# The loop of a gated attention-and-expert kernel, turned: the next tile's scores first, then q, u and the output

## The chip, the cores and the metric

The kernel runs on one core of one Trainium2 chip. The metric is the device time of one execution in microseconds (us). A core has five engines that each work through their own instructions in order: TensorE (PE in the profile; its weight loads are PEld), VectorE (DVE), ScalarE (ACT), GpSimd (POOL) and SyncE (SP, which here only issues DMAs). They wait for one another through semaphores. The tile library inserts those waits from the data that instructions share, and from the reuse of buffers; in this kernel each engine's order is the order in which the program writes its instructions.

## The reference

Two branches over the same input x (2048 rows of 512) are mixed by a gate per row.

```
g = sigmoid((x * gate_w).sum(-1))
# A: linear attention, 32 heads of 16
q, k, v = heads(x @ wqkv)
phi(y)  = concat(softmax(y @ w_phi), softmax(-(y @ w_phi)))      # 32 features per head
kv, z   = phi(k)^T v, sum over rows of phi(k)
a       = (phi(q) kv / (phi(q) z + 1e-6)) @ wo
# B: 32 heads, each picks one of 256 experts
s1, s2  = scores of x with 2 x 16 keys per head
e       = argmax(s1) * 16 + argmax(s2)
b       = sum over heads of gelu(x . u[e]) * v[e]                # softmax over one candidate is 1
out     = g * a + (1 - g) * b
```

## The kernel before, in words

Rows are handled in 16 tiles of 128. Matrix products are made of three products of a high and a low part each (`mm3`, L51 to L56), so a 128x512 output with 512 inputs takes 12 matmuls.

The first part of the program (to L336) projects k and v for every tile, takes the softmax features of k and sums up kv and z. It also folds the expert keys into the score weights (`sh`, `sl`) and `w_phi` into the q weights. The last lines of it already compute the scores of tile 0. kv and z of the last two tiles are finished after it, v of the last two tiles only in the second iteration of the loop.

The second part is the loop over tiles. One tile t goes through these steps, spread over three iterations:

- `front_s` (L225): the scores, two halves of 12 matmuls (tiles `s`).
- `best` (L441): VectorE finds the maximum of each head's 16 scores and marks where it is (`mx`, `eq`, L447 and L448). `turn_eq` (L451) has SP issue a DMA that transposes the marks (`et`).
- `mid_mask` (L505): 8 small matmuls turn the marks into bit masks. `count` (L515) is a chain of 17 steps on VectorE that counts, for each of the 256 experts, how many heads picked it (L519 to L553). It is a generator: `step(t, n)` issues its next n steps, `drain(t)` the rest, so that the chain can be laid between other instructions.
- `front_q` (L386): q with `w_phi` in it, 12 matmuls (`pq`). `soft_in` (L391) makes the four VectorE operations of `softmax_diffs` (L90 to L96), `soft_exp` (L400) the exp in two halves on ScalarE (L403), `soft_w` (L405) the products with z on GpSimd (`w`, L409), `soft_sum` and `soft_y` the sums over each head's features on VectorE (L413 and L417), and `soft_b` (L419) the small operations that end in one factor per feature group (L423 to L433), with a `step` of the count behind each of them, and the scaling of the features by it on GpSimd (`d`, L439).
- `planes` (L467) and `join` (L477): the scaled features are transposed by two DMAs per tile, on 16-bit halves: ScalarE splits (`pl`, L472), SP issues the transposes (`tp`), ScalarE joins (`pt`, L482).
- `front_p` (L350): x with all 256 expert vectors u and with the gate vector, 12 matmuls of 258 columns (`pp`). `gelu_pre` (L356), `gate`, `gelu_in`, `gelu_act`, `gelu_out`: gelu and gate on ScalarE, VectorE and GpSimd. `coef` (L555) multiplies the count with it (`cf`).
- `mid_num` (L485) and `num_lo`: the numerator from `pt` and kv, with its high and low part (`oh`, `ol`). `back_c` (L559) and `back_cl`: transposes of the coefficients (`CT`, `ch`, `cl`).
- `back_o`, `back_ol`, `back_out` (L573 to L595): the output product of 18 matmuls over `wo` and the expert vectors v (`po`). `store` copies it and issues its DMA.

PSUM gives the products two rotating sets: four buffers `mm` (scores, q, u, coefficient transposes, output) and three `tr` (numerator, masks). A product has to wait until the one four places earlier in its set has been read.

In the order before, iteration a of the loop (L642) handles tile z = a-2 in its numerator and output, b = a-1 in its transposes and the rest of its count, a in its q and softmax, and n = a+1 in its scores and u. TensorE's order in it is: numerator of z, coefficient transposes of z, q of a, output of z, masks of a, scores of n, u of n. The last tile's q and the last outputs are written out behind the loop (L710 to L758).

The weights `wo` are loaded and split into `wbh` and `wbl` in the second iteration, because these two buffers hold the weights of v until then (L669, L690, L701 and L706).

Of the kernel before, what the change touches and what calls it, by code (L numbers as in the profile page):

```python
# [33 lines left out]
def mix_kernel(ctx, tc, xT, wqT, wkT, wv, wphi, wo, wq, kk, ug, ev, cst, out):  # L34
# [306 lines left out]
    def step(t, n=1):  # L341
        for _ in range(n):
            if t in chains and next(chains[t], None) is None:
                del chains[t]

    def drain(t):
        while t in chains:
            step(t)

    def front_p(t, evict=True):  # L350
        pp = st8[t]["pp"] = mm_bank(f"pp{t}")
        proj(pp[:, :NU], t, uh, ul, 0, NU)
        if evict:
            gelu_pre(t)

    def gelu_pre(t):  # L356
        pp = st8[t]["pp"]
        gs = w2.tile([P, 4], F32, name=f"gs{t}", tag="gs")
        act.activation(gs[:, 0:1], pp[:, NX:NX + 1], AF.Exp, scale=-1.0)
        act.activation(gs[:, 1:2], gs[:, 0:1], AF.Copy, bias=1.0)  # L360
        px = w2.tile([P, NX], F32, name=f"px{t}", tag="px")
        x2 = w2.tile([P, NX], F32, name=f"x2{t}", tag="x2")
        act.copy(px, pp[:, :NX])
        act.activation(x2, pp[:, :NX], AF.Square)
        act.activation(x2, x2, AF.Copy, bias=GELU_C, scale=0.044715 * GELU_C)
        st8[t].update(g=gs, G=px, x2=x2)

    def gate(t):
        gs = st8[t]["g"]
        yield dve.reciprocal(gs[:, 2:3], gs[:, 1:2])  # L370

    def gelu_in(t):
        px, x2 = st8[t]["G"], st8[t]["x2"]
        pool.tensor_tensor(x2, x2, px, op=ALU.mult)

    def gelu_act(t):
# [3 lines left out]
        act.activation(x2, x2, AF.Identity, bias=gs[:, 3:4], scale=gs[:, 3:4])  # L380
# [19 lines left out]
    def soft_exp(t):  # L400
        d = st8[t]["ph"]
        for s_ in halves:
            act.activation(d[:, s_], d[:, s_], AF.Exp)  # L403
# [63 lines left out]
    def planes(t):  # L467
        e = st8[t]
        e["tp"] = []
        for i, s_ in enumerate(halves):  # L470
            pl = w3.tile([P, 2, 512], U16, tag="pl", name=f"pl{i}_{t}")
            act.copy(pl, e["ph"][:, s_].bitcast(U16).rearrange("p (c j) -> p j c", j=2))  # L472
# [32 lines left out]
    def mid_mask(t):  # L505
        e = st8[t]
        o = tr_bank(f"mk{t}")[:, :64]
        for half in range(2):
            for w in range(2):
                for q in range(2):  # L510
                    pe.matmul(o[:, half * 32 + w * F:half * 32 + w * F + F], e["et"][:, half * 4 + w * 2 + q, :],
                              wm[:, q, :], start=(q == 0), stop=(q == 1))
        chains[t] = count(t, o)
# [100 lines left out]
    def z_final():  # L614
        for j in range(2):
            o = mm_bank(f"z{j}")
            for g in range(4):
                pe.matmul(o[:, g * P:(g + 1) * P], zc[:, 4 * j + g:4 * j + g + 1].to_broadcast([P, P]), ident,
                          start=True, stop=True)
            act.copy(zb[:, 512 * j:512 * j + 512], o)  # L620

    def wo_load(ks):
        for k in ks:
            rawo[k] = w3.tile([P, D], F32, tag="ot", name=f"rawo{k}")
            sp.dma_start(rawo[k], wo[:, k, :])

    rawo = {}
    kvz(NT - 2)
    best(0, 0)
    best(0, 1)  # L630
    cb.close()
    w3 = ctx.enter_context(tc_pool("w3", "left"))
    turn_eq(0)
    front_q(0)
    soft_in(0)
    front_p(0, False)
    kvz(NT - 1)
    act.copy(zc, acc[:, :, F])
    gelu_pre(0)
    z_final()  # L640
    wo_load((0, 1))
    for a in range(NT - 1):  # L642
        n, b, z = a + 1, a - 1, a - 2
        B, Z = b >= 0, z >= 0
        if Z:
            mid_num(z)
            back_c(z)
        if B:
            planes(b)
            front_q(a)  # L650
        if a == 1:
            v14, v15 = vproj(NT - 2), vproj(NT - 1)
        gelu_in(a)
        if Z:
            num_lo(z)
            back_cl(z)
        for _ in gate(a):
            step(b)
        gelu_act(a)
        if B:  # L660
            step(b, 4)
            soft_in(a, lambda: step(b, 2))
            drain(b)
        if a == 1:
            v14()
        soft_exp(a)
        if a == 1:
            v15()
            for k in range(2):  # L669
                act.copy(wbh[:, k, :], rawo[k])  # L670
        if Z:
            back_o(z)
            back_ol(z)
            back_out(z)
            store(z)
        mid_mask(a)
        front_s(n, 0)
        if a == 1:
# [4 lines left out]
        front_s(n, 1)  # L683
        front_p(n, False)
        soft_w(a)
        soft_sum(a, 0)
        soft_sum(a, 1)
        if a == 1:
            for k in range(2):
                pool.tensor_tensor(wbl[:, k, :], rawo[k], wbh[:, k, :], op=ALU.subtract)  # L690
            wo_load((2, 3))
        best(n, 0)
        soft_y(a, 0)
        soft_y(a, 1)
        if B:
            join(b)
            gelu_out(b)
            coef(b)
        if a == 1:
            kv_final()  # L700
            for k in range(2, NK):  # L701
                act.copy(wbh[:, k, :], rawo[k])
        soft_b(a)
        if a == 1:
            for k in range(2, NK):
                pool.tensor_tensor(wbl[:, k, :], rawo[k], wbh[:, k, :], op=ALU.subtract)  # L706
        best(n, 1)
        turn_eq(n)
        gelu_pre(n)
    a, b, z = NT - 1, NT - 2, NT - 3  # L710
    mid_num(z)
    back_c(z)
    planes(b)
    front_q(a)
    gelu_in(a)
    gelu_out(b)
    num_lo(z)
    back_cl(z)
    for _ in gate(a):
        step(b)  # L720
    gelu_act(a)
    step(b, 4)
    soft_in(a, lambda: step(b, 2))
    drain(b)
    coef(b)
    back_o(z)
    back_ol(z)
    join(b)
    soft_exp(a)
    back_out(z)  # L730
    store(z)
    mid_mask(a)
    soft_w(a)
    soft_sum(a, 0)
    soft_sum(a, 1)
    mid_num(b)
    back_c(b)
    num_lo(b)
    back_cl(b)
    soft_y(a, 0)  # L740
    soft_y(a, 1)
    gelu_out(a)
    soft_b(a)
    back_o(b)
    back_ol(b)
    back_out(b)
    mid_phi(a)
    store(b)
    drain(a)
    coef(a)  # L750
    mid_num(a)
    num_lo(a)
    back_o(a)
    back_c(a)
    back_cl(a)
    back_ol(a)
    back_out(a)
    store(a)  # L758


def _consts():
# [49 lines left out]
```

## Time and profile before

| | us |
|---|---|
| median of three executions (389.7 to 391.84) | 389.85 |
| profiled execution | 389.51 |
| its span, first to last instruction | 387.7 |
| PE busy | 379.2 (98%) |
| DVE busy | 324.3 (84%) |
| ACT busy | 214.2 (55%) |
| POOL busy | 155.9 (40%) |
| DMA | 45.38 MB, mean 117 GB/s |

The profile is one execution of the program, recorded by the hardware. A row of a timeline gives the start in us from the span's beginning, the duration, the engine, the program's line, the operation, the tile that it writes and those that it reads, and how many instructions were merged; in brackets stands how long the engine sat idle before it and what released it. Rows of windows give the length of a stretch, then each engine's busy time with the number of instructions, the granted TensorE clock as a share of the full one, and the DMA's share and rate. Matmuls are pipelined, so a row's duration is longer than the distance to the next.

### The profile page before, as it was taken

How to read it: one execution, taken by the hardware profiler on the slowest of the kernel's cores; microseconds unless marked ns; L12 is line 12 of the kernel's file. 1: busy time of each engine (PE TensorE's matmuls, PEld its weight loads, DVE VectorE, ACT ScalarE, POOL GpSimd, SP SyncE). 2: the span in 40 equal slices, each digit the busy share in tenths (PEclk: the TensorE clock that was granted, in tenths of full speed). 3: DMA queues.
4: the chain of work that ended last, by engine and by line, in shares of the span. 5: the costliest groups of instructions: out<-in, count | busy, mean ns of one | idle time of the engine just before them, and what ended most of it. 6: DMA issues, size and time to landing. Idle time of an engine off the chain costs nothing.

```text
span 387.7 us, 9193 instructions
## 1 busy us (share of the span) xinstructions
PE 379.2 (98%) x3688; PEld 296.4 (76%) x3688; DVE 324.3 (84%) x798; ACT 214.2 (55%) x390; POOL 155.9 (40%) x165
## 2 busy tenths in 40 slices
PE   8999999999999999999999999999999999999975
PEld 4866787777768888877878878888888788888753
DVE  4358866866868969889999999999999999999994
ACT  4335555644646345758548458557656664674732
POOL 1005435325326233936426426336335344364350
PEclk9999999999999999999999999999999999999989
DMA  7489787487692033143252231331440431322301
GB/s 272 157 257 313 210 254 231 142 227 238 199 300 57 16 71 81 61 78 81 57 83 60 77 81 50 88 83 34 104 83 28 90 84 48 81 69 69 83 28 56
DMA packets 66715, 45.38 MB, mean 117 GB/s; under 512 B 58096, under 2 KB 58992, under 8 KB 64368
## 3 DMA queue, kind: packets, MB, share of 16 engines
q1 hardware_dynamic: 65808, 43.92, 41.5%
q10 hardware_dynamic: 864, 0.87, 0.8%
q8 instruction: 29, 0.48, 0.5%
q14 instruction: 14, 0.11, 0.1%
HBM read 26.43 MB, written 4.19 MB: 79 GB/s over the span
## 4 chain that ended last, share of the span: by engine, by line
PE 83%; DVE 8%; ACT 3%; DMA 2%; POOL 2%; issue 1%; ACTq 0%; POOLq 0%
PE s L54 7%; PE s L56 6%; PE s L55 6%; PE pk L54 4%; PE ws L204 4%; PE pk L55 4%; PE pk L56 4%; PE pv L54 4%; PE po L578 4%; PE po L579 4%; PE po L584 3%; PE pv L55 3%; PE pv L56 3%; PE pq L54 3%; PE pq L56 3%; PE pq L55 3%
## 5 line engine op out<-in xcount | busy, mean ns | idle before, releaser
L409 POOL TENSOR_TENSOR w<-d,zb 128x512 f32<-128x512 f32 x32 | 40.8, 1299 | 94.6 <-ACT d L403 94.6
L181 POOL TENSOR_TENSOR d<-d,st 128x1024 f32<-128x1024 f32 x16 | 31.0, 1939 | 74.5 <-DVE st L180 38.4
L54 PE MATMUL s<-sh,xh 128*128 128x512 f32 x128 | 51.8, 405 | 0.0
L56 PE MATMUL s<-sh,xl 128*128 128x512 f32 x128 | 50.0, 391 | 0.0
L55 PE MATMUL s<-sl,xh 128*128 128x512 f32 x128 | 49.9, 390 | 0.0
L403 ACT ACTIVATE d<-d 128x512 f32<-128x512 f32 x32 | 18.4, 624 | 56.9 <-DVE d L96 56.9
L439 POOL TENSOR_TENSOR d<-d,st 128x512 f32<-128x512 f32 x31 | 32.7, 1077 | 25.6 <-DVE st L433 20.8
L482 ACT COPY pt<-tp 128x1024 uint16<-128x1024 uint16 x30 | 39.0, 1368 | 1.5 <-DMA tp<-pl 0.9
L326 ACT ACTIVATE d<-d 128x1024 f32<-128x1024 f32 x16 | 17.0, 1063 | 27.9 <-DVE d L96 27.9
L472 ACT COPY pl<-d 128x1024 uint16<-128x1024 uint16 x30 | 30.5, 1061 | 1.6 <-POOL d L439 1.4
L56 PEld LDWEIGHTS s<-sh,xl 128*128 128x128 f32 x128 | 24.0, 188 | 5.4
L413 DVE TENSOR_REDUCE st<-d 128x32 f32<-128x512 f32 x32 | 20.5, 681 | 8.9 <-ACT d L403 8.9
L54 PEld LDWEIGHTS s<-sh,xh 128*128 128x128 f32 x128 | 24.0, 188 | 4.6
L55 PEld LDWEIGHTS s<-sl,xh 128*128 128x128 f32 x128 | 24.1, 188 | 4.5
L578 PE MATMUL po<-wbh,oh 128*128 128x512 f32 x64 | 26.4, 412 | 0.8 <-ACT oh L496 0.8
L54 PE MATMUL pv<-wbh,xh 128*128 128x512 f32 x64 | 26.3, 411 | 0.2 <-ACT wbh L48 0.2
L54 PE MATMUL pq<-wah,xh 128*128 128x512 f32 x64 | 26.5, 415 | 0.0
L579 PE MATMUL po<-wbl,oh 128*128 128x512 f32 x64 | 26.2, 409 | 0.0
L55 PE MATMUL pv<-wbl,xh 128*128 128x512 f32 x64 | 25.4, 396 | 0.2 <-DVE wbl L49 0.2
L179 DVE TENSOR_REDUCE st<-d 128x64 f32<-128x1024 f32 x16 | 19.5, 1218 | 7.0 <-ACT d L326 7.0
L54 PE MATMUL pk<-wah,xh 128*128 128x512 f32 x64 | 25.3, 395 | 0.0
L56 PE MATMUL pv<-wbh,xl 128*128 128x512 f32 x64 | 25.2, 394 | 0.0
(147 smaller groups left out, 1019.9 us busy)
## 6 DMA issues: line engine op xcount, KB each, us to landing
wq<-wq SPq DMA_DIRECT2D x16, 1024.0 KB, 5.9
xr<-xT SPq DMA_DIRECT2D x15, 256.0 KB, 6.1
y<-ot SPq DMA_DIRECT2D x15, 256.0 KB, 2.0
rawk<-wkT SPq DMA_DIRECT2D x1, 1024.0 KB, 6.5
rawq<-wqT SPq DMA_DIRECT2D x1, 1024.0 KB, 4.8
rawo<-wo SPq DMA_DIRECT2D x4, 256.0 KB, 3.7
rawu<-ug SPq DMA_DIRECT2D x2, 258.0 KB, 6.0
rawv<-wv ACTq DMA_DIRECT2D x2, 256.0 KB, 4.6
```

The costliest lines, as they stand in the source:

```text
L54: pe.matmul(o, ah, bh, start=(first and i == 0), stop=False)
L55: pe.matmul(o, ah, bl, start=False, stop=False)
L56: pe.matmul(o, al, bh, start=False, stop=(last and i == n - 1))
L179: dve.tensor_reduce(st[:, 64:128], g64(d), axis=AX.X, op=ALU.add)
L181: pool.tensor_tensor(g64(d), g64(d), b64(st[:, 128:192]), op=ALU.mult)
L409: pool.tensor_tensor(e["w"][:, s_], e["ph"][:, s_], zb[:, s_], op=ALU.mult)
L413: dve.tensor_reduce(e["st"][:, 64 + 32 * i:96 + 32 * i], g64(e["ph"])[:, 32 * i:32 * i + 32], axis=AX.X, op=ALU.add)
L439: eng.tensor_tensor(g64(d)[:, gs_], g64(d)[:, gs_], r[:, gs_].unsqueeze(2).to_broadcast([P, 32, F]), op=ALU.mult)
L472: act.copy(pl, e["ph"][:, s_].bitcast(U16).rearrange("p (c j) -> p j c", j=2))
L482: act.copy(p16[:, :, 4 * i:4 * i + 4, :], e["tp"][i].rearrange("p (j g) n -> p j g n", j=2))
L578: pe.matmul(po, oh[:, k, :], wbh[:, k, :], start=(k == 0), stop=False)
L579: pe.matmul(po, oh[:, k, :], wbl[:, k, :], start=False, stop=False)
```

## The change

The order of the calls in the loop is rewritten; no operation on the tiles is added or left out. There is one loop over all 16 tiles, k, with z = k-2, b = k-1 and n = k+1. TensorE's order in an iteration becomes: numerator of z, coefficient transposes of z, masks of k, scores of n, q of k, u of k, output of z. Thus u is computed in the iteration of q, one later than before, and the output is last.

On VectorE, the iteration begins with `soft_b` of b, which had ended the iteration before it, and with the last steps of b's count. The count of k is placed behind the two calls of `best`: 7 steps after the first, 5 after the second, and the last 5 between the operations of `soft_b` in the next iteration. q's differences have no steps between them any more, and nothing stands between the sums of the exp and those over w but the gate's reciprocal before the last one. On GpSimd, `gelu_in`, `gelu_out` and `coef` of b follow the scaling of b's features, and `w` of k comes last. On ScalarE, `join` of b comes before the exp of k, and `gelu_pre` of k after it.

In the first iteration the sums for z (`kvz`, `z_final`) come after scores, q and u. The first half of `wo` is split in iteration 1 behind `join`, the second half in iteration 2 behind `join`. The last iteration has no scores; it takes `join` behind the exp, with four count steps ahead of it.

```diff
+    def back(t):
+        back_o(t)
+        back_ol(t)
+        back_out(t)
+        store(t)
+
+    def wo_split(ks):
+        for k in ks:
+            act.copy(wbh[:, k, :], rawo[k])
+            pool.tensor_tensor(wbl[:, k, :], rawo[k], wbh[:, k, :], op=ALU.subtract)
+
     rawo = {}
-    kvz(NT - 2)
     best(0, 0)
     best(0, 1)
...
-    for a in range(NT - 1):
-        n, b, z = a + 1, a - 1, a - 2
-        B, Z = b >= 0, z >= 0
+    for k in range(NT):
+        n, b, z = k + 1, k - 1, k - 2
+        B, Z, N, last = b >= 0, z >= 0, n < NT, k == NT - 1
         if Z:
             mid_num(z)
             back_c(z)
         if B:
+            mid_mask(k)
+        if N:
+            front_s(n, 0)
+            front_s(n, 1)
+        if B:
+            soft_b(b)
+            drain(b)
             planes(b)
-            front_q(a)
...
+            gelu_in(b)
+            gelu_act(b)
         if Z:
             num_lo(z)
             back_cl(z)
-        for _ in gate(a):
-            step(b)
-        gelu_act(a)
         if B:
-            step(b, 4)
-            soft_in(a, lambda: step(b, 2))
-            drain(b)
-        if a == 1:
+            gelu_out(b)
+            coef(b)
+        if k == 1:
+            v14, v15 = vproj(NT - 2), vproj(NT - 1)
             v14()
...
+            kv_final()
+        front_q(k)
+        if N:
+            best(n, 0)
+            step(k, 7)
+            best(n, 1)
+            turn_eq(n)
+            step(k, 5)
+        else:
+            step(k, 2)
+        front_p(k, False)
+        if k == 0:
+            kvz(NT - 2)
+            kvz(NT - 1)
+            mid_mask(0)
+        if B and not last:
+            join(b)
+        if k == 1:
+            wo_split((0, 1))
             wo_load((2, 3))
...
+        if k == 2:
+            wo_split((2, 3))
+        soft_in(k)
+        soft_exp(k)
+        if k == 0:
+            step(0, 12)
+            act.copy(zc, acc[:, :, F])
+            z_final()
+        if last:
+            step(k, 4)
             join(b)
...
+        gelu_pre(k)
+        soft_w(k)
+        soft_sum(k, 0)
+        soft_sum(k, 1)
+        soft_y(k, 0)
+        for _ in gate(k):
+            pass
+        soft_y(k, 1)
+        if Z:
+            back(z)
+    a, b = NT - 1, NT - 2
     mid_num(b)
     back_c(b)
+    gelu_in(a)
+    gelu_act(a)
     gelu_out(a)
     soft_b(a)
     back_o(b)
+    num_lo(b)
+    back_cl(b)
     mid_phi(a)
     drain(a)
     coef(a)
+    back_ol(b)
     mid_num(a)
+    back_c(a)
+    back_out(b)
+    store(b)
     num_lo(a)
     back_cl(a)
+    back(a)
```

More of the change, by code (lines that the diff above doesn't have):

```diff
@@ L633, in mix_kernel @@
     turn_eq(0)
[L634 to L640, printed above, removed]
     wo_load((0, 1))
-    for a in range(NT - 1):
-        n, b, z = a + 1, a - 1, a - 2
-        B, Z = b >= 0, z >= 0
+    for k in range(NT):
+        n, b, z = k + 1, k - 1, k - 2
+        B, Z, N, last = b >= 0, z >= 0, n < NT, k == NT - 1
         if Z:
@@ L648, in mix_kernel @@
         if B:
+            mid_mask(k)
[5 more added lines that the diff above has]
+            drain(b)
             planes(b)
-            front_q(a)
-        if a == 1:
-            v14, v15 = vproj(NT - 2), vproj(NT - 1)
-        gelu_in(a)
+            gelu_in(b)
+            gelu_act(b)
         if Z:
@@ L656, in mix_kernel @@
             back_cl(z)
-        for _ in gate(a):
-            step(b)
-        gelu_act(a)
         if B:
-            step(b, 4)
-            soft_in(a, lambda: step(b, 2))
-            drain(b)
-        if a == 1:
+            gelu_out(b)
+            coef(b)
+        if k == 1:
+            v14, v15 = vproj(NT - 2), vproj(NT - 1)
             v14()
-        soft_exp(a)
-        if a == 1:
             v15()
[L669 to L678, printed above, removed]
             kvacc(NT - 2)
@@ L682, in mix_kernel @@
             w4 = ctx.enter_context(tc_pool("w4", "right"))
[L683 to L690, printed above, removed]
-            wo_load((2, 3))
[L692 to L695, printed above, removed]
-            join(b)
[L697 to L735, printed above, removed]
+            kv_final()
[13 more added lines that the diff above has]
+            mid_mask(0)
@@ L736, in mix_kernel @@
+        for _ in gate(k):
[4 more added lines that the diff above has]
+    a, b = NT - 1, NT - 2
     mid_num(b)
     back_c(b)
[L738 to L741, printed above, removed]
+    gelu_in(a)
+    gelu_act(a)
     gelu_out(a)
@@ L744, in mix_kernel @@
     back_o(b)
-    back_ol(b)
-    back_out(b)
+    num_lo(b)
+    back_cl(b)
     mid_phi(a)
-    store(b)
     drain(a)
     coef(a)
+    back_ol(b)
     mid_num(a)
+    back_c(a)
+    back_out(b)
+    store(b)
     num_lo(a)
-    back_o(a)
-    back_c(a)
     back_cl(a)
-    back_ol(a)
-    back_out(a)
-    store(a)
+    back(a)
 def _consts():
```

## The prediction, made before the changed kernel ran

> **What bounds the kernel now.** I read the page's engine totals, then a window of one iteration, then the chain of work that ended last.
>
> ```profile
> span 387.7 us, 9193 instructions
> PE 379.2 (98%) x3688; PEld 296.4 (76%) x3688; DVE 324.3 (84%) x798; ACT 214.2 (55%) x390; POOL 155.9 (40%) x165
> ...
> 337.02:352.16 15.14, 15.14 (x109) 12.31 (x110) 14.13 (x42) 9.18 (x18) 6.77 (x7) 1.00 0.30 70
> ...
> PE 83%; DVE 8%; ACT 3%; DMA 2%; POOL 2%; issue 1%; ACTq 0%; POOLq 0%
> ```
>
> The third row is one iteration, from the first score product of one to that of the next: length, then busy time of PE, PEld, DVE, ACT, POOL, and behind them the granted clock. TensorE has no gap in it, and the last row, the chain's shares, puts 83% of the span on TensorE. The second number to see is VectorE's 14.13 of 15.14: the next engine has about 1 us to spare. The change adds and removes no arithmetic, so TensorE's work of 15.14 per iteration stays. A new order can only change how long TensorE idles at the start and in the tail, or push a round of another in-order engine above 15.14. So I worked out VectorE's round. Its timeline in one iteration before, with the two rows of ScalarE and GpSimd that it waits for:
>
> ```profile
> 321.94 0.68 DVE L96 TENSOR_TENSOR d<-st,pq 128x512 f32<-128x512 f32 x1
> ...
> 323.32 1.28 DVE L413 TENSOR_REDUCE st<-d 128x32 f32<-128x512 f32 x2 [0.36 <-ACT d L403]
> 324.79 0.69 DVE L447 TENSOR_REDUCE mx<-s 128x32 f32<-128x512 f32 x1 [0.19 <-PE s L56]
> ...
> 326.12 1.27 DVE L417 TENSOR_REDUCE st<-w 128x32 f32<-128x512 f32 x2
> 327.31 0.54 DVE L423 RECIPROCAL st<-st 128x64 f32<-128x64 f32 x1
> ...
> 328.96 0.19 DVE L523 TENSOR_TENSOR sa<-sb 128x64 uint16<-128x64 uint16 x1
> 329.06 0.69 DVE L447 TENSOR_REDUCE mx<-s 128x32 f32<-128x512 f32 x1
> ...
> 330.62 0.76 DVE L503 TENSOR_TENSOR ol<-oT,oh 128x256 fp32r<-128x256 f32 x2
> ...
> 331.69 0.37 DVE L527 TENSOR_TENSOR m<-sa 128x32 uint16<-128x32 uint16 x2
> ...
> 332.71 0.29 DVE L542 TENSOR_SCALAR T<-X 128x256 uint32<-128x256 uint32 x1
> ...
> 333.71 0.68 DVE L90 TENSOR_REDUCE st<-pq 128x32 f32<-128x512 f32 x1
> 334.31 0.28 DVE L545 TENSOR_SCALAR X<-X 128x256 uint32<-128x256 uint32 x1
> ...
> 322.65 1.16 ACT L403 ACTIVATE d<-d 128x512 f32<-128x512 f32 x2 [3.73 <-DVE d L96]
> ...
> 323.36 2.56 POOL L409 TENSOR_TENSOR w<-d,zb 128x512 f32<-128x512 f32 x2 [6.60 <-ACT d L403]
> ```
>
> The reader is to see a latency that is partly covered. The last difference of q ends at 322.62; the exp starts 0.03 later, the first sum of its result 0.70 later (323.32), and GpSimd's products w end at 325.92, which is 3.30 after 322.62. Before, the last count step and best(n,0) (L447 and L448, 324.79 to 326.12) fill that time, so the sums over w (326.12) wait for nothing.
>
> **The change, part by part.** *TensorE's order* becomes num, coefficient transposes, masks, scores of the next tile, q, u, output. Same matmuls, so 0 by itself.
>
> *VectorE's round* (from one L423 to the next) is where I see the cost. The count no longer runs between q's differences, and best(n,0) no longer stands between the sums and the w sums. By start-to-start distances:
> (a) soft_b with count steps 13 to 17 in it. Soft_b with steps 1 to 5 takes 1.75 (327.31 to 329.06). The later steps are longer; alone they take 1.70 in the tail:
>
> ```profile
> 377.20 0.29 DVE L542 TENSOR_SCALAR T<-X 128x256 uint32<-128x256 uint32 x1
> ...
> 379.11 0.29 DVE L547 TENSOR_TENSOR T<-X 128x256 uint16<-128x256 uint16 x1
> ...
> 380.81 0.42 DVE L557 TENSOR_TENSOR cf<-cf,px 128x256 f32<-128x256 f32 x1
> ```
>
> Bounds 1.75 and 1.75+1.70-0.5 = 2.95 (0.5 being five of the 0.10 from 328.96 to 329.06). I take 2.25: two chains that fill each other's latencies, as in the row they replace.
> (b) num_lo and back_cl, 1.00 of the 1.07 from 330.62 to 331.69.
> (c) best twice, 2 x 1.33 = 2.66.
> (d) count steps 1 to 7 with nothing between: the five small ones cost 0.5 (pipelined at 0.10) to 1.3 (1.75 less 0.46 for L423, as if they were all of it). I take 1.0, dependent operations of under 0.2 each; steps 6 and 7 are 331.69 to 332.71, 1.02. Together 2.0.
> (e) steps 8 to 12 alone, 377.20 to 379.11, less 0.1 where best's end overlaps: 1.8.
> (f) q's four differences without steps between, 4 x 0.60 (333.71 to 334.31), to the end of the last: 2.48.
> (g) from there 3.30 to the end of w, 0.05 to react and 0.60 for the last w sum: 3.95. Only 2.5 of it is work (two sums 1.2, two w sums 1.2, the gate's reciprocal); about 1.45 is idle, where 0.36 was before.
> Sum: 2.25+1.00+2.66+2.0+1.8+2.48+3.95 = **16.14**, already 1.0 above TensorE's 15.14.
>
> *What GpSimd adds to that.* In the second iteration before, GpSimd runs beside count steps:
>
> ```profile
> 159.15 0.69 DVE L425 TENSOR_TENSOR st<-st 128x64 f32<-128x64 f32 x1
> 159.77 0.74 DVE L520 TENSOR_TENSOR sb<-sa 128x64 uint16<-128x64 uint16 x1
> ...
> 193.05 0.19 DVE L520 TENSOR_TENSOR sb<-sa 128x64 uint16<-128x64 uint16 x1
> ...
> 159.71 0.75 POOL L384 TENSOR_TENSOR px<-x,px 128x256 f32<-128x256 f32 x1
> ...
> 329.12 2.08 POOL L439 TENSOR_TENSOR d<-d,st 128x512 f32<-128x512 f32 x2 [1.68 <-DVE st L433]
> ```
>
> L520 takes 0.74 until just after GpSimd's product ends (160.46), against 0.19 when GpSimd is idle. In the new round soft_b comes first, so GpSimd's two halves of d (2.08) and gelu_in (of L384's size, 0.75) run from 2.0 (or 2.3, if the last count step holds them) to 5.2 after its start, and steps 2 to 7 begin at about 4.9 (a+b+one best+one step): about 0.3 more. Bounds 0 and 1.0, two whole products. **Round 16.4**; bounds 15.6 (a at 2.0, d at 1.55, no blocking) and 17.2.
>
> The Trainium skill ("SBUF — State Buffer", SBUF: two separate sides) says that VectorE and GpSimd share one port pair as an exclusive lock, held for a whole instruction, by a VectorE operation with two SBUF inputs or in a two-port mode. The rows above agree for two inputs. By that rule the one-input step 8 would also wait for GpSimd's coefficient product, some 0.25 more per round by the 0.74 rows, which no row here shows; the sum would be 414 with it.
>
> *What stands behind.* If VectorE is late by 1.2 each iteration, TensorE waits: the next scores take the PSUM buffer of q, free only when q's differences are done. ScalarE and SP hold no longer loop:
>
> ```profile
> 331.01 2.02 ACT L472 COPY pl<-d 128x1024 uint16<-128x1024 uint16 x2
> ...
> 333.47 0.60 ACT L380 ACTIVATE x<-x,gs 128x256 f32<-128x256 f32 x1
> ...
> 324.18 2.60 ACT L482 COPY pt<-tp 128x1024 uint16<-128x1024 uint16 x2
> ...
> tp<-pl SPq DMA_TRANSPOSE x4, 2.8
> ```
>
> Planes start 3.4 after soft_b's start, the transpose of the first half lands 1.0+2.8 later, join takes 2.6: done at about 10, while the exp queued behind it is due at 12.2 (a to f). It is hidden; with that cover of 2 gone it would add what it exceeds.
>
> *The start.*
>
> ```profile
> 137.57 0.47 PE L54 MATMUL s<-sh,xh 128*128 128x512 f32 x1
> ...
> 143.09 0.28 PE L54 MATMUL pp<-uh,xh 128*128 128x258 f32 x1
> ...
> 144.51 0.40 PE L54 MATMUL pq<-wah,xh 128*128 128x512 f32 x1
> ...
> 152.77 0.36 PE L511 MATMUL mk<-wm,et 128*128 128x16 bf16 x8
> ...
> 155.95 1.27 PE L188 MATMUL kvacc<-v,d 128*32 128x16 f32 x128
> ...
> 164.02 2.57 POOL L706 TENSOR_TENSOR wbl<-rawo,wbh 128x512 fp32r<-128x512 f32 x2
> ...
> 192.33 0.55 DVE L423 RECIPROCAL st<-st 128x64 f32<-128x64 f32 x1
> ```
>
> Before, TensorE has done q(1), v14 and v15 at 152.77. In the new order q(1) comes after scores(2) (5.52, from 137.57 to 143.09), a mask and both kv sums too, less u(1) (1.42): 152.77+5.52+0.2+1.3-1.42, and 0.9 waiting for the z copy, now queued behind an exp: 159.3. VectorE idles for it some 4 us. q's differences end at 161.8. GpSimd's two wo remainders (2.57) now stand before w in both k=1 and k=2 and hold it up by about 0.9 and 0.65; so the L423 of tile 1 is at 166.65, of tile 2 at 183.7. The first output product waits for wo's second half, split only behind join(1), until about 180, TensorE idling some 8 us; that delays scores(4) by 0 to 2 beyond VectorE's need, I take 0.9. The L423 of tile 3 falls at 201.0, against 192.33.
>
> *The tail.*
>
> ```profile
> 357.60 0.55 DVE L423 RECIPROCAL st<-st 128x64 f32<-128x64 f32 x1
> ...
> 373.02 0.54 DVE L423 RECIPROCAL st<-st 128x64 f32<-128x64 f32 x1
> ```
>
> Before, from the L423 of tile 14 to that of 15 takes 15.4, and 14.7 more to the end, 30.1 together. New: no scores, so q's differences end 6.1 after the first; but w waits behind gelu_out and coef on GpSimd. These follow the planes and gelu on ScalarE (3.06 from 331.01 to 334.07, so until 6.6) and take two 0.75, to 8.2; w ends at 10.8, and the last sum at 11.4; 11.9 with steps blocked beside it. From the last L423 the old 14.7, and 1.2 because the last coefficient transposes and tile 14's six closing matmuls now precede the whole last output product: 15.9. Together 27.8, a gain of 2.3.
>
> *Sum.* 201.0 + 11 x 16.4 + 27.8 = 409.2 of span. The profiled execution took 389.51 for 387.7, so 1.8 outside: **411**. It lies 0.34 under the median of the runs shown, which changes nothing here.
>
> **Rivals.** (1) *Count steps hide better*: round 15.6, the low bound. For it: soft_b's 0.10 steps. Against: the steps are a chain with nothing between them now. 411 - 11 x 0.8 = 402.
> (2) *GpSimd blocks more*: one more whole product of 0.74 per round, since gelu_out and coef fall beside steps 7 and 8. 411 + 11 x 0.75 = 419.
> (3) *TensorE's clock drops in the new gaps.*
>
> ```profile
> 370.65:374.00 3.35, 3.35 (x9) 2.62 (x10) 3.24 (x11) 0.50 (x2) 2.42 (x3) 0.55 0.21 81
> ```
>
> The granted clock there is 0.55, after TensorE's sparse stretch before. 3.35 x 0.45 = 1.5 lost per drop makes TensorE's round 16.65 plus reaction, say 16.8: 415. Against: the gaps are 1.2 long and the granted clock of the iteration row is 1.00. The Trainium skill ("TensorE: Matmul & The Clock Gate", Part 1) has the clock halve after an idle window of about 3.4 us; by it neither gap of 1.2 would trip it, and the tail's row agrees with a drop after a longer quiet stretch.
> (4) *TensorE stays the bound* (the other side): VectorE's round comes to 15.14 or less. Place: (d) and (g); price: 1.26 a round; point: round 15.14. Then TensorE's own work sets the end: tile 13's output product, before one iteration behind 352.16 at about 367.1, comes later only by what TensorE idles at the start, 1.1 (z) to 9.5 (with the wait for wo). From there it is 17.3 by the tail's terms (q(15) is done 5.8 earlier, then 2.5+4.3+15.9, rounded up by 0.4 for the reaction), and 1.8 outside: 387 to 396, middle 391.5, no longer slower by more than 0.5% below 5.6 of idling. For it: VectorE's 14.13. Against: (g)'s idle 1.45 comes on top.
>
> **How the numbers follow.** Forecast 53%, rival 1 20%, rival 2 12%, rival 3 5%, rival 4 10%. The range 397 to 420 leaves out most of rival 4 and a little above rival 2. A measurement of this kernel tells 0.5% (2 us) from no change. Faster and same come from rival 4 alone, its 387 to 391.8, half of its chance, and as much again for errors of the start in rivals 1 and 4: 0.05 and 0.06; slower 0.89.
>
> **What would show it.** In the profile after: TensorE's first score product waiting about 1 us per iteration for L96; L417 waiting for w, L413 for the exp with 0.7; iterations 16 to 17 long; DVE near 14.5 busy in them; L520 long where L374 runs; an 8 us gap before the first L578. Wrong if iterations are 15.1 with TensorE gapless, or if the waits before L417 are missing.

## The result, and the profile after

The changed kernel takes **412.65 us** (median of four executions, 411.29 to 413.34); the kernel before, run beside it, takes 389.77. The ratio is 1.057 with a 95% interval of 1.0525 to 1.0616. The profiled execution took 412.62 for a span of 410.8, which is 23.1 longer than before.

The page of the changed kernel: span and instructions, busy time of each engine, the TensorE clock in 40 slices of the span, and the shares of the chain that ended last.

```profile
span 410.8 us, 9252 instructions
PE 385.3 (94%) x3688; PEld 299.3 (73%) x3688; DVE 329.9 (80%) x798; ACT 216.4 (53%) x390; POOL 156.5 (38%) x165
...
PEclk9999999999999989969999999999999999999969
...
DVE 42%; PE 37%; POOL 10%; issue 3%; DMA 3%; ACT 3%; ACTq 0%; POOLq 0%; DVEq 0%
```

The instructions of the engines are the same in number, but TensorE has fallen from 83% of the chain to 37%, and VectorE leads it with 42%. The clock row is full in the loop and drops only near the middle (the start of the loop) and in the last slices.

To see where the 23.1 us went, I cut both spans at the same two events: the reciprocal L423 of tile 3 and that of tile 14. Windows of the kernel before between these two (busy time of PE, PEld, DVE, ACT and POOL, then the granted clock):

```profile
192.33:357.60 165.27, 165.27 (x1178) 134.08 (x1177) 155.88 (x452) 101.34 (x198) 74.78 (x78) 1.00 0.31 71
```

The same stretch after, and one typical round of it:

```profile
204.57:380.38 175.81, 170.30 (x1203) 137.98 (x1201) 157.10 (x453) 103.16 (x198) 75.41 (x77) 1.00 0.35 67
284.34:300.29 15.95, 15.28 (x110) 12.41 (x109) 14.25 (x42) 9.49 (x18) 6.85 (x7) 1.00 0.32 67
```

Up to tile 3 the changed kernel loses 12.24 (204.57 against 192.33), in the eleven rounds 10.54 (175.81 against 165.27), and behind them 0.32 (410.8 - 380.38 = 30.42 against 30.1). A round takes 15.98 on average, in which TensorE idles 0.50 and VectorE 1.70 (175.81 - 157.10 over 11). VectorE was idle 0.85 per round before (165.27 - 155.88 over 11), so 0.85 of the 0.96 by which a round is longer is new idle time of VectorE.

VectorE's timeline in the typical round, from one L423 to the next:

```profile
284.34 0.54 DVE L423 RECIPROCAL st<-st 128x64 f32<-128x64 f32 x1
...
286.41 0.75 DVE L503 TENSOR_TENSOR ol<-oT,oh 128x256 fp32r<-128x256 f32 x2
...
287.40 0.68 DVE L447 TENSOR_REDUCE mx<-s 128x32 f32<-128x512 f32 x1
...
288.72 0.21 DVE L519 CAST sa<-mk 128x64 uint16<-128x64 f32 x1
...
290.73 0.69 DVE L447 TENSOR_REDUCE mx<-s 128x32 f32<-128x512 f32 x1
...
292.06 0.34 DVE L542 TENSOR_SCALAR T<-X 128x256 uint32<-128x256 uint32 x1
...
293.89 0.68 DVE L90 TENSOR_REDUCE st<-pq 128x32 f32<-128x512 f32 x1
...
295.69 0.67 DVE L96 TENSOR_TENSOR d<-st,pq 128x512 f32<-128x512 f32 x1
297.06 1.28 DVE L413 TENSOR_REDUCE st<-d 128x32 f32<-128x512 f32 x2 [0.70 <-ACT d L403]
298.44 0.69 DVE L417 TENSOR_REDUCE st<-w 128x32 f32<-128x512 f32 x1
...
299.69 0.69 DVE L417 TENSOR_REDUCE st<-w 128x32 f32<-128x512 f32 x1 [0.49 <-POOL w L409]
300.29 0.55 DVE L423 RECIPROCAL st<-st 128x64 f32<-128x64 f32 x1
```

The reader is to see two idle stretches, 0.70 ahead of L413 and 0.49 ahead of the second L417. Both stand in the latency from q's last difference over the exp and GpSimd's products back to VectorE, which nothing on VectorE fills any more. The sums of all such waits between 200 and 370 us (in total, times, longest):

```profile
DVE st L413 <- ACT d L403: 7.7, 11, 0.7
DVE st L417 <- POOL w L409: 5.4, 11, 0.5
PE s L54 <- DVE d L96: 3.1, 5, 0.7
```

The first two come in every round; the third is TensorE's first score product, which waits for the buffer that q's differences free. It comes in only 5 of the 11: TensorE enters these rounds ahead of VectorE, and its first score products follow one another by 15.10 up to 233.08, then by about 16. VectorE is late, and TensorE waits for it once its lead is used up.

### The profile page after: what moved, and what is told of

Same layout as the page of the kernel before. It is cut to its first block, busy times and chain, and to the rows that moved or that the text cites. A ratio compares the mean times of both kernels' runs of the same rounds, so it can differ in the third digit from the quotient of the medians.

```text
span 410.8 us, 9252 instructions
## 1 busy us (share of the span) xinstructions
PE 385.3 (94%) x3688; PEld 299.3 (73%) x3688; DVE 329.9 (80%) x798; ACT 216.4 (53%) x390; POOL 156.5 (38%) x165
## 4 chain that ended last, share of the span: by engine, by line
DVE 42%; PE 37%; POOL 10%; issue 3%; DMA 3%; ACT 3%; ACTq 0%; POOLq 0%; DVEq 0%
POOL w L409 8%; DVE eq L448 4%; PE pv L54 4%; DVE mx L447 4%; PE ws L204 3%; PE pk L54 3%; PE pv L55 3%; PE pk L55 3%; PE pk L56 3%; PE pv L56 3%; DVE st L417 2%; ACT d L403 2%; DVE ol L503 2%; DVE st L90 2%; DVE d L96 2%
## 5 line engine op out<-in xcount | busy, mean ns | idle before, releaser
L578 PE MATMUL po<-wbh,oh 128*128 128x512 f32 x64 | 27.1, 423 | 4.9 <-ACT wbh L635 4.2
L417 DVE TENSOR_REDUCE st<-w 128x32 f32<-128x512 f32 x32 | 21.9, 684 | 9.1 <-POOL w L409 7.9
L413 DVE TENSOR_REDUCE st<-d 128x32 f32<-128x512 f32 x32 | 20.4, 680 | 9.8 <-ACT d L403 9.8
L579 PE MATMUL po<-wbl,oh 128*128 128x512 f32 x64 | 27.1, 423 | 0.6 <-POOL wbl L636 0.6
L54 PE MATMUL pq<-wah,xh 128*128 128x512 f32 x64 | 25.4, 398 | 0.4 <-DVE d L96 0.4
```

The lines of the kernel that those rows point to most:

```text
L54: pe.matmul(o, ah, bh, start=(first and i == 0), stop=False)
L417: dve.tensor_reduce(e["st"][:, 192 + 32 * i:224 + 32 * i], g64(e["w"])[:, 32 * i:32 * i + 32], axis=AX.X, op=ALU.add)
```

## The experiments

**Fill the exp's latency.** Two of the five count steps behind `best(n, 1)` are put between q's differences and the sums of the exp.

```diff
-            step(k, 5)
+            step(k, 3)
...
         soft_in(k)
         soft_exp(k)
+        if N:
+            step(k, 2)
```

> Two of the five count steps that stand ahead of q's differences (L545 and L546, 0.67 us together in the profile after) move behind them, into the 0.70 us in which VectorE waits for the exp. Theory, VectorE's own round sets the pace and its idle time counts in full: the round falls from 15.96 by 0.67 to 15.3 us, over some 12 rounds 8 us, about 404.6 in all. Rival, the pace is set elsewhere (TensorE with a lowered clock, GpSimd, a transfer): no change, 412.6.

Measured: 404.46 (403.27 to 405.41), ratio to before 1.0363 (1.0337 to 1.0389), span 401.5. Its window between the same two events, and its VectorE timeline at the place of the edit:

```profile
203.50:371.11 167.61, 167.61 (x1197) 137.09 (x1196) 156.09 (x452) 103.19 (x199) 75.21 (x77) 1.00 0.34 70
```

```profile
290.60 0.29 DVE L545 TENSOR_SCALAR X<-X 128x256 uint32<-128x256 uint32 x1
290.93 0.43 DVE L546 TENSOR_TENSOR X<-X,T 128x512 uint16<-128x512 uint16 x1
291.39 1.28 DVE L413 TENSOR_REDUCE st<-d 128x32 f32<-128x512 f32 x2
```

L413 waits for nothing here, and eleven rounds take 167.61 instead of 175.81, so 15.24 each, with TensorE busy throughout (its own iterations take 15.10). Putting 0.79 us of existing work (290.60 to 291.39) back into the gap gave 8.2 us between the two events. Most of the 13.8 us of span that stay against the kernel before lie ahead of tile 3 (203.50 against 192.33); 2.34 lie in the eleven rounds.

**Fill the latency of the products w instead.** The same two steps stand between `soft_sum` and `soft_y`.

```diff
-            step(k, 5)
+            step(k, 3)
...
         soft_sum(k, 1)
+        if N:
+            step(k, 2)
         soft_y(k, 0)
```

> The same two count steps move to the place between the sums of the exp and the first sum over w, where VectorE waits 0.1 and 0.5 us for GpSimd's products. If only idle time counts, about 0.5 us of a round is saved, 6 us in all, 406 to 407. If VectorE's step and GpSimd's product exclude each other (the products run there back to back, 1.28 us each), the second step ends only with the second product, the sums over w follow late by 0.65, and nothing is gained: 412 to 413.

Measured: 415.2 (414.81 to 416.03), ratio 1.0643 (1.0621 to 1.0664): no gain, and the eleven rounds are 1.28 longer (177.09). VectorE at that place:

```profile
299.60 1.40 DVE L546 TENSOR_TENSOR X<-X,T 128x512 uint16<-128x512 uint16 x1
300.92 0.67 DVE L417 TENSOR_REDUCE st<-w 128x32 f32<-128x512 f32 x1
```

L546 takes 1.40 against 0.43 elsewhere, because it runs beside a product of GpSimd (w, 298.12 to 300.72), and the sums over w stand behind it. The gap is there, but only work that can run beside GpSimd fits into it.

**An operation that does fit.** The reciprocal of the sums, first of `soft_b`, is moved ahead of the first sum over w.

```diff
+    def soft_r(t):
+        st = st8[t]["st"]
+        dve.reciprocal(st[:, 128:192], st[:, 64:128])
...
-        dve.reciprocal(r, sm)
         step(t)
...
         soft_sum(k, 1)
+        soft_r(k)
         soft_y(k, 0)
```

> The reciprocal of the sums (L423, 0.46 us of the round) moves from behind the sums over w to the place ahead of them. It reads one small tile. Theory: it fills the 0.6 us of waiting for w, the round falls by 0.46 to 15.5 us, 5.5 us in all, about 407. If a reciprocal too has to wait for GpSimd's products, it ends up to 1.2 later and nothing is gained: 412 or more.

Measured: 406.38 (405.9 to 406.94), ratio 1.0413 (1.0389 to 1.0436), span 404.8. The reciprocal (L421 here) beside GpSimd's w:

```profile
294.03 0.56 DVE L421 RECIPROCAL st<-st 128x64 f32<-128x64 f32 x1
...
295.34 0.69 DVE L417 TENSOR_REDUCE st<-w 128x32 f32<-128x512 f32 x1
```

Its duration is about that of L423 (0.54), although w runs on GpSimd from 292.76 to 295.31, and the wait before the second L417 is down from 0.49 to 0.14. The eleven rounds take 171.33 (200.75 to 372.08), 15.58 each; the expectation's 15.5 held within 0.1. They make 4.48 of the 6.0 by which the span is shorter; the other 1.5 lie ahead of tile 3 and behind tile 14.

**Less work for TensorE.** This kernel leaves out the four products L584 of every tile but tile 14, so the numerator's low part is missing from the output; it shows only whether TensorE sets the pace.

```diff
     def back(t):
         back_o(t)
-        back_ol(t)
         back_out(t)
```

> The four matmuls of the numerator's low part (L584) are left out of every output product, 0.93 us of TensorE's time per tile; the output loses the part that they compute. Theory, VectorE sets the pace: the rounds of the loop stay at 15.96, only the last tiles save about 1 each, 410 to 412. Rival, TensorE sets the pace in some hidden way: 0.93 less in each of 13 rounds, about 400.

Measured, one execution: 411.6, span 409.8.

```profile
203.36:379.12 175.76, 164.23 (x1155) 130.90 (x1154) 157.10 (x452) 102.86 (x198) 75.34 (x77) 0.98 0.35 67
```

TensorE is busy 6 us less than in the changed kernel, and the eleven rounds take 175.76 against 175.81. The pace is not TensorE's.

**The lost cover alone, in the kernel before.** In the old order `best(n, 0)` is moved from ahead of the sums over w to behind them; nothing else changes.

```diff
-        best(n, 0)
         soft_y(a, 0)
         soft_y(a, 1)
+        best(n, 0)
```

> The kernel before with one line moved: the first half of best goes from ahead of the sums over w to behind them, so nothing covers GpSimd's products. VectorE's free round there is 14.87 (L96 from 187.25 to 202.12); it gains waits of 0.15 and 0.7, which makes 15.7, above TensorE's 15.14. Theory: 0.55 in some 13 rounds, 395 to 398. Rival, the cover is worth nothing since TensorE hides it: 389.8.

Measured: 401.21 (399.82 to 401.65), ratio 1.028 (1.0255 to 1.0304), span 398.0. VectorE at the place:

```profile
303.10 0.69 DVE L417 TENSOR_REDUCE st<-w 128x32 f32<-128x512 f32 x1 [0.57 <-POOL w L409]
303.70 0.68 DVE L447 TENSOR_REDUCE mx<-s 128x32 f32<-128x512 f32 x1
```

The same wait appears in the old order (0.57), and the round is 15.72 (172.92 us from 195.01 to 367.93 for eleven), the 15.7 that was expected. TensorE, which had no gap in these rounds, now idles 3.3 us in them. Moving one operation out of the gap turned a kernel bound by TensorE into one bound by VectorE. The time came out 3 us above the expectation, because the start lost too: tile 3's L423 stood at 195.01 against 192.33.

**The start, twice.** The first attempt takes the z sums ahead of q(0) and splits wo earlier. The second takes only the z copy and products ahead of the exp of tile 0, computes v of tiles 14 and 15 in iteration 0, and puts the last two kv sums between the score halves of iteration 1, with wo again split earlier and twelve count steps of tile 0 moved behind its sums. The core of the second:

```diff
         if N:
             front_s(n, 0)
+            if k == 1:
+                kvacc(NT - 2)
+                kvacc(NT - 1)
...
+                kv_final()
             front_s(n, 1)
...
+            act.copy(zc, acc[:, :, F])
             mid_mask(0)
+            zo = z_mm()
+            v14, v15 = vproj(NT - 2), vproj(NT - 1)
```

> Two waits of the start are taken away: the sums for z and their products go ahead of the exp of tile 0, and the second half of wo is split in iteration 1 behind w, the first half ahead of join. Theory: the start costs what VectorE loses by them, 2.4 at z, 0.7 and 0.3 of waiting for w in iterations 1 and 2, 1.8 of waiting for scores 4; about 4 to 5 us, 408. If the rounds of VectorE hide the start, no change, 412.6.

> Only the start of the changed kernel is rearranged, second attempt: the copy of the z sums and the z products move ahead of the exp of tile 0, v of tiles 14 and 15 is computed in iteration 0 behind them (its copies behind the exp and the first gelu step, so that nothing queues behind planes(0)), the last two kv sums stand between the two score halves of iteration 1, so that q of tile 1 has none of them ahead of it; the first half of wo is split ahead of join(0), the second half behind the w products of iteration 1; twelve count steps of tile 0 come behind the sums of tile 0. Theory (the start costs some 3 to 4 us beyond the rounds, through q of tile 1 coming late, the remainders of wo ahead of w, and the first output waiting for wo): the reciprocal L423 of tile 1 falls at about 167 instead of 169.7, that of tile 3 at about 201 instead of 204.6, no wait of VectorE for q of tile 1, rounds stay 15.96: 409 to 410. Rival (as in the first attempt, what one engine gains at the start another one loses): L423 of tile 3 at 203 to 204.6, 411.5 to 412.6.

Measured: 412.44 (412.12 to 412.72) and 412.19 (410.8 to 413.9). Neither is told apart from the changed kernel, so both theories missed and the times of both rivals held. In the first, the kv sums waited 3.92 for copies of v that stood on ScalarE behind the planes. In the second, q(1) was there in time, but tile 1's L423 came at 169.53 all the same. GpSimd and VectorE in its second iteration:

```profile
160.29 2.65 POOL L640 TENSOR_TENSOR wbl<-rawo,wbh 128x512 fp32r<-128x512 f32 x2
...
160.51 1.28 DVE L545 TENSOR_SCALAR X<-X 128x256 uint32<-128x256 uint32 x1
161.82 1.40 DVE L546 TENSOR_TENSOR X<-X,T 128x512 uint16<-128x512 uint16 x1
163.14 0.68 DVE L90 TENSOR_REDUCE st<-pq 128x32 f32<-128x512 f32 x1
```

Count steps 8 to 12 take 4.6 (158.56 to 163.14) instead of 1.83: the earlier remainders of wo run beside the last two of them (shown), `gelu_out` and `coef` beside the others. What TensorE's earlier q gave, VectorE lost behind GpSimd. So the theory on where the start loses (q of tile 1) had the wait right and the gain wrong: the wait was replaced at once.

**The tail.** The four count steps ahead of `join` in the last iteration are left where `drain` takes them later.

```diff
         if last:
-            step(k, 4)
             join(b)
```

> The four count steps ahead of the last sums are left to the later places of the count. In the profile after they wait for GpSimd's products one by one and the sums of the last tile begin 3 us late, while w itself is there at 390.8. Theory: the last L423 comes 1.9 earlier, at 391.4 after the start, and the end by 1 to 1.9, 411 to 411.6. Rival: the same steps come back on the path to the last coefficients, 412.6 or more.

Measured: 410.31 (409.88 to 410.7), ratio 1.0519 (1.0498 to 1.0539). From tile 14's L423 to tile 15's it took 11.10 instead of 12.89, but from there to the end 18.37 instead of 17.53: the steps come later, not free. The net is 0.95, at the low end of what the theory gave; 1.25 more of the profile's difference is an earlier tile 14, which the edit doesn't reach.

**Together.** The two edits of the round, the shortened last iteration and the first version of the start; then the same with the second version.

> Both fills (two steps behind q's differences, the reciprocal ahead of the sums over w), the start's two changes and the tail's one. VectorE's round by the theory: 15.96 - 0.67 - 0.46 = 14.8, below TensorE's 15.14, so TensorE sets the pace again. 11 x 0.84 = 9 less for the rounds, 4.5 for the start, 1.5 for the tail: about 397. If the parts do not add up, 400 to 405.

> The combination of four edits again (two count steps in front of the sums of the exp, the reciprocal ahead of the first product over w, the shortened last iteration) with the second version of the start in place of the first. Theory: the rounds are TensorE's again (15.10 per iteration), so that what TensorE idles at the start reaches the end: without the idle 4.84 for the copies of v and with wo earlier some 4 to 6 us less than 397.0: 391 to 393, and not below 389.8 beyond the measurement, because TensorE's work is that of the kernel before. Rival: the idle time of the start is only moved to another wait, 395 to 397.

Measured: 397.0 (395.56 to 398.48), ratio 1.0176 (1.0149 to 1.0203), then 392.43 (391.85 to 394.71), ratio 1.0067 (1.0042 to 1.0091). The second combination's window between the two events (L421 there), and the shares of its chain:

```profile
197.17:359.91 162.74, 162.74 (x1138) 133.36 (x1137) 156.28 (x451) 103.47 (x199) 75.45 (x79) 1.00 0.36 72
```

```profile
DVE 41%; PE 38%; POOL 9%; ACT 4%; DMA 4%; issue 2%; ACTq 0%; DVEq 0%; POOLq 0%
```

The first combination's 397 is the expected number, but not by the expected sum: the eleven rounds gave 12.8 (163.0 instead of 175.81) where 9 had been taken, and the start lost where 4.5 had been hoped for (q's differences of tile 1 begin at 167.24 instead of 162.67). In the second, the rounds are 14.79 on VectorE. TensorE has no gap in them, but its own iterations take 15.10 (first score products from 195.73 to 346.73, ten iterations): VectorE comes out of the start late and catches up by 0.3 a round. The second version of the start is 4.6 us better than the first here: TensorE no longer idles 4.84 for the copies of v as in the first combination, and the two steps that stood beside the remainders of wo now come behind q's differences, which begin at 161.52 instead of 163.14. The expected iterations of 15.10 and the time held. But the expectation named TensorE alone as the bound, and the chain still goes mostly through VectorE; the runs don't tell which of them sets the last microsecond. No run has the combined rounds with the changed kernel's own start, so what the second version is worth by itself stays open.

**The ends of that version.** Three more edits: z sums ahead of u of tile 0; the first gelu step and the gate of tile 15 behind tile 14's numerator; tile 14's closing products ahead of the last coefficient transposes. The output of tile 13 moves behind the loop with them, its store behind tile 14's numerator.

```diff
-    mid_num(b)
-    back_c(b)
+    back_o(b - 1)
+    back_ol(b - 1)
+    back_out(b - 1)
+    mid_num(b)
+    back_c(b)
+    store(b - 1)
+    gelu_pre(a)
...
     mid_num(a)
-    back_c(a)
     back_out(b)
     store(b)
+    back_c(a)
```

> The second combination with three more edits, all where its TensorE stood idle at the two ends. Start: the last two z sums come ahead of u of tile 0, so that the z products find their copy done (idle 1.07 at 144.85 in the second combination). Tail: the first gelu step of tile 15 and its gate come behind the numerator of tile 14 (ScalarE reached the high part oh late by it: idle 0.76 and 1.18 of TensorE up to 373.68, followed by a granted clock of 0.62 in the stretch 374 to 378), and the six closing products of tile 14 come ahead of the last coefficient transposes (idle 1.33 at 381.07). Theory (TensorE sets the pace between the ends, so that what it idles less there arrives in the time): about 1.0 + 1.2 + 1.2 less, 389 to 389.5, and up to 1.5 less again if the granted clock holds: a tie with the kernel before, or just below it. Rival (the count of tile 15 on VectorE sets the end, its coefficients being done at 381.0 whatever TensorE does): the tail keeps its length, 391 to 392.5.

Measured: 393.2 (391.84 to 394.15), ratio 1.0071 (1.0047 to 1.0095). This is not told apart from the second combination, and neither theory nor rival held: the tail did not shorten, nor keep its length. From tile 15's L421 to the end it takes 21.8 instead of 20.6: the gate came late (VectorE idle 1.39 for it), and with it the scaling of tile 15's features, so that TensorE waited for those 2.15 and 1.22 instead. The last coefficients came 12.2 after that L421 instead of 10.6. Nor did the start gain: L421 of tile 3 stands at 197.63 against 197.17. No version run here is faster than the kernel before.

## Why the prediction was right, step by step

The sign, the engine and the place were as predicted, and the time of 411 was 1.65 below the measurement. That closeness is luck, resting on errors that offset one another: on the span, the start was 3.6 longer than worked out (204.57 against 201.0), the eleven rounds 4.6 shorter (175.81 against 180.4), the tail 2.6 longer (30.42 against 27.8).

**The round** by the terms of the sum, read from the timeline of the typical round:

| term | predicted | measured |
|---|---|---|
| (a) soft_b with steps 13 to 17 | 2.25 | 2.07 |
| (b) num_lo and back_cl | 1.00 | 0.99 |
| (c) best, twice | 2.66 | 2.65 |
| (d) steps 1 to 7 | 2.0 | 2.01 |
| (e) steps 8 to 12 | 1.8 | 1.83 |
| (f) q's differences | 2.48 | 2.47 |
| (g) exp, w and the sums | 3.95 | 3.93 |
| sum | 16.14 | 15.95 |
| beside GpSimd | 0.3 | 0.03 (the mean of the eleven rounds, 15.98, less this one) |

The seven terms held; the furthest off is (a), by 0.18. That the idle time of (g) is the cause is shown from both sides: filling its wait for the exp in the new order took 0.74 off the round and left TensorE without a gap, and uncovering its wait for w in the old order brought that wait there. The mis-sized term is **the 0.3 for GpSimd**. In the second iteration before, L520 had begun with GpSimd's product; here it begins at that product's end. GpSimd and VectorE beside each other after the change, first in a typical round, then in iteration 0:

```profile
288.39 0.73 POOL L374 TENSOR_TENSOR x<-x,px 128x256 f32<-128x256 f32 x1
...
291.51 0.74 POOL L557 TENSOR_TENSOR cf<-cf,px 128x256 f32<-128x256 f32 x1
...
145.36 1.26 POOL L409 TENSOR_TENSOR w<-d,zb 128x512 f32<-128x512 f32 x1 [10.48 <-ACT zb L620]
```

```profile
288.97 0.21 DVE L520 TENSOR_TENSOR sb<-sa 128x64 uint16<-128x64 uint16 x1
...
145.42 1.35 DVE L544 TENSOR_SCALAR T<-X 128x256 uint32<-128x256 uint32 x1
...
308.00 0.64 DVE L542 TENSOR_SCALAR T<-X 128x256 uint32<-128x256 uint32 x1
```

L520 starts 0.15 before L374 ends and takes 0.21. The one-input step 8 (L542) takes 0.34 in the typical round, where the coefficient product ends 0.19 after its start, and 0.64 in the one round where that product came later; alone it takes 0.29. The Trainium skill ("SBUF — State Buffer", SBUF: two separate sides) has a one-input VectorE operation in a two-port mode take the same lock as a two-input one. The trace agrees as far as it goes: L544, with one input, takes 1.35 beside w against 0.29 alone; the mode that it runs in is in no row. The 414 by that rule didn't come about, because the operations hardly overlap, not because the rule fails.

**The start.** The q(1) that was predicted at 159.3 came at 162.67. Of these 3.4, 1.5 were there before the loop's order matters (kv sums of tile 13 at 130.40 against 128.87; in the variants of the new order, where that part is unchanged, at 129.1 to 130.7). The idle 0.91 ahead of the z products had been counted. The rest came with them: the granted clock fell to 0.64 for 3.61 us and was 0.86 in the next 3.00, some 1.7 us lost by estimate (3.61 x 0.36 + 3.00 x 0.14). VectorE's wait for q(1) was 2.12, not 4, as VectorE was late itself. The wait for wo ended when predicted (180.16) and was half of the 8 us in size; it stood inside the output product, behind its first four matmuls. Its clock was not in the prediction:

```profile
162.67 0.69 DVE L90 TENSOR_REDUCE st<-pq 128x32 f32<-128x512 f32 x1 [2.12 <-PE pq L56]
...
180.16 0.80 PE L578 MATMUL po<-wbh,oh 128*128 128x512 f32 x1 [4.22 <-ACT wbh L635]
181.51 0.80 PE L579 MATMUL po<-wbl,oh 128*128 128x512 f32 x1 [0.56 <-POOL wbl L636]
...
190.78 0.69 DVE L447 TENSOR_REDUCE mx<-s 128x32 f32<-128x512 f32 x1 [1.82 <-PE s L56]
```

```profile
143.39:147.00 3.61, 3.61 (x26) 3.45 (x27) 3.37 (x11) 1.25 (x4) 1.29 (x2) 0.64 0.02 5
...
180.16:184.00 3.84, 3.26 (x6) 1.84 (x7) 2.81 (x6) 2.69 (x8) 3.81 (x4) 0.50 0.00 0
```

After the gap the granted clock is 0.50 for 3.84 us. The Trainium skill ("TensorE: Matmul & The Clock Gate", Part 1) has the clock halve after an idle window of about 3.4 us, and the 4.22 of idle time agrees. I had used that rule only against a drop in the loop, where it held, and had not applied it to the 8 us gap that I predicted myself. VectorE then waited 1.82 for scores(4), where 0.9 had been taken.

**The tail.** The step that failed is "coef to 8.2, w ends at 10.8", with only 0.5 for steps blocked beside it, and the 15.9 behind the last L423. VectorE in tiles 14 and 15 after the change, then the last coefficient transposes on TensorE, in the kernel before and in the changed one:

```profile
380.38 0.54 DVE L423 RECIPROCAL st<-st 128x64 f32<-128x64 f32 x1
...
388.40 2.43 DVE L527 TENSOR_TENSOR m<-sa 128x32 uint16<-128x32 uint16 x2
...
393.27 0.54 DVE L423 RECIPROCAL st<-st 128x64 f32<-128x64 f32 x1
```

```profile
381.29 0.44 PE L563 MATMUL CT<-cs,cf 128*128 128x128 f32 x2
...
401.31 0.44 PE L563 MATMUL CT<-cs,cf 128*128 128x128 f32 x2 [0.86 <-DVE cf L557]
```

GpSimd runs gelu_out, coef and both halves of w without a pause from 386.73 to 390.78, and two short operations of one count step (L527) hold VectorE until it is done; only then come the sums. From L423 to L423 it took 12.89 instead of 11.9.

The rest took 17.53 against 15.9. Up to the last coefficient transposes it is 8.04 (393.27 to 401.31), no longer than the 8.27 before (373.02 to 381.29). Behind them it is 9.49 against 6.41, so 3.08 more, where the prediction took 1.2: **that 1.2 is the mis-sized term**. The prediction counted tile 14's six closing matmuls, but the eight `oh` products of the last output (L578 and L579), which ran ahead of the transposes before (379.28 to 381.29), now stand behind them too; in the chain after, the fourteen take 3.26 (401.74 to 405.00).

TensorE also waits 4.60 for tile 14's `pt` (L491 at 390.11), which stood behind the exp, and its granted clock is 0.50 from 393.30 to 397.00. The sum had neither, but nothing shows that they cost time at the end: the chain that ended last goes through VectorE from 380.46 to 401.26, and TensorE waits 0.86 for the coefficients at its end.

**The rivals and the signs.** The mean round of 15.98 lies between rival 1's 15.6 and the forecast's 16.4, as far from one as from the other; rival 1's 402 was wrong because start and tail were longer than the sum that it shares with the forecast. (The terms named for its 15.6, a at 2.0 and d at 1.55, give 15.44.) Rival 2 (more blocking) had the wrong sign. Rival 3's clock drops came, but in the start and the tail, not in the loop. Rival 4 was ruled out by the kernel with less work for TensorE. Of the signs, the waits ahead of L413 (0.70) and L417 (0.49) came in every round; TensorE's wait for L96 was at most 0.7 and came in 5 of 11; a round is just under the 16 to 17 named, with VectorE 14.25 busy instead of 14.5; L520 was not long in it.

## What to carry to other kernels

A schedule bound by one engine can hide that the next one lives on a cover: before moving an operation, ask which latency it stands in, and sum the other engine's round by start-to-start distances with that latency empty. Here the seven terms so worked out agreed to 0.2 us. In these runs, work put into the wait for a busy neighbour paid only where it was of a kind that could run beside it, and removing a wait at the start paid nothing where another engine's wait took its place at once.

## What the runs showed of the hardware that was not expected

The kinds of VectorE operations part sharply beside GpSimd's w: a reciprocal and tensor_reduce run at their usual length (0.56 and 0.69), while a tensor_scalar and a tensor_tensor of 16- or 32-bit integers wait for the end of the running product (1.35 and 1.40 against 0.29 and 0.43). Back to back products leave gaps for a single operation: L527, two operations of together 0.30, took 2.43.

The granted clock fell to 0.64 in the window from 143.39, shown above, where TensorE had not been idle for long. Its timeline ahead of it:

```profile
140.94 1.25 PE L196 MATMUL kvacc<-ones,d 128*32 128x1 f32 x128
142.12 0.36 PE L511 MATMUL mk<-wm,et 128*128 128x16 bf16 x8
143.39 0.82 PE L618 MATMUL z<-cs,zc 128*128 128x128 f32 x5 [0.91 <-ACT zc L702]
```

The wait was 0.91, behind 1.5 us of products of one and of 16 columns. In the kernel before, the same z products came behind a wait of 0.28, at a granted clock of 1.00, and took 2.05 instead of 2.88. The row that the prediction shows from the tail before (0.55 from 370.65) is such a case too: in the 3.75 us ahead of it TensorE is busy 1.68, and its longest wait is this one:

```profile
369.95 0.44 PE L563 MATMUL CT<-cs,cf 128*128 128x128 f32 x2 [1.56 <-POOL cf L557]
```

So that row shows no single long wait ahead of the drop, though the prediction took it for a long quiet stretch; the 4.22 for wo is one. Whether small products count as idle for the clock was not tried.
